# State decays without a biasing product in a recurrent-attention kernel: exponentials on each half of the rows, and a new order of work

## The chip, the core and the metric

The kernel runs on one core of one Trainium2 chip. A core has TensorE (PE), VectorE (DVE), ScalarE (ACT), GpSimd (POOL), and SyncE (SP), which here issues the DMAs. Time is device time in microseconds (us) of one launch; lower is better. Three runs of the kernel before gave 182.21, 182.34 and 183.43 us, a median of 182.34.

## What is computed

A linear attention with data-dependent decay (4 batches, 8 heads, 768 positions, 48 numbers per head), then a mixing layer with two Fourier transforms, a normalization and a two-layer MLP:

```
for t in range(S):
    cur = einsum('bhd,bhe->bhde', u * k[t], v[t])
    y[t] = einsum('bhd,bhde->bhe', r[t], state + cur)
    state = w[t][..., None] * state + einsum('bhd,bhe->bhde', k[t], v[t])

X = fft(fft(x, axis=1), axis=2)            # x: y with the heads side by side, 384 wide
u = x + real(X)
un = (u - mean(u)) / sqrt(var(u) + 1e-6)
out = u + relu(un @ w_ch1) @ w_ch2         # 384 -> 1536 -> 384
```

## The kernel before

**Tiles.** A batch is cut into six chunks of 128 positions, written (batch, chunk) below. For each chunk the tensors w, k, r and v are loaded as 128 x 384 tiles (four loads, 192 KB each, seven buffers per tensor). The logarithm of w (`L`, ACT) is summed along the positions by matmuls with a triangular mask (L799, and L822 for a second kind of sum), and exponentials of these sums scale r and k (L853 on DVE for r, L884 for k). Both are transposed, by PE and an evicting copy (L899, L911), or by a transposing DMA on SP's queue (L889). Then come the scores (L922), a mask (L932), the product with v and with the carried state (L984, L987), and the sum with a diagonal part (L998 on DVE, or L1007 as an fp32 product on PE in batch 0).

**State decay.** Between chunks the state is multiplied by the product of w over the whole chunk, one number per head and feature. The state tile holds two heads stacked: rows 0 to 63 belong to the even head of each of four pairs, rows 64 to 127 to the odd one. `total` makes the exponents in a 128 x 8 strip beside the sums: four small matmuls of `L` with a column of ones (L813) give each pair's sums in two columns, and ahead of them one product of the identity with `PB` (L810, the biasing product) puts -200 into the half that belongs to the other head. The exponential of the strip is then the decay where it belongs, and 0 elsewhere, and can be used as a per-row factor (L967, or L972 and L975 where the state stays in PSUM). In the way `sum_two` the strip lies next to the sums, and one exponential (L826) covers both; in `sum_add` and `sum_key` it has an exponential of its own (`decays`, L831). The last chunk of a batch has no decay.

**Mixing and MLP.** The Fourier transforms are matmuls with tables (L1063 to L1068, then L1107 or L1116). The normalized rows go, transposed, through the MLP in two halves of a batch: L1235 with W1, evicted by ACT or DVE with a ReLU (L1243, L1241), and L1254 with W2, then a last DVE instruction (L1263) and the store (L1274).

**Order.** Every operation is registered with a number; where a step can be done in several ways (`choose`), all of them are registered. `ORDER` lists for each engine which numbers run, in which sequence, and so which way and which engine each step has. An engine works strictly in that sequence. A planner with a cost for each operation laid the lists out; at build time its costs decide only which PSUM bank a tile gets and which waits are written first. 32 warming products (L1321), whose results nobody reads, stand in PE's list as filler. The MLP of one batch is interleaved with the attention of the next ones.

Of the kernel before, what the change touches and what calls it, by code (L numbers as in the profile page):

```python
# [8 lines left out]
ACTF = mybir.ActivationFunctionType  # L9
# [30 lines left out]
        "7 2638 2639 2640 2641 72 98 100 153 101 154 68 151 66 64 123 125 2642 180 181 130 206 183 137 204 "  # L40
        "207 147 200 257 233 259 260 148 190 234 201 243 286 2643 236 287 322 2644 323 320 289 248 296 2645 "
        "2646 437 382 306 2647 384 349 350 2648 402 359 404 352 2649 307 2650 409 438 2651 363 2652 451 452 "
        "2653 2654 2655 2656 695 697 642 698 416 2657 465 453 439 724 750 466 644 645 467 440 2658 468 471 "
        "443 474 446 477 725 2659 478 479 480 483 486 491 454 457 460 503 751 497 498 504 492 505 530 499 "
        "2660 671 2661 493 531 672 2662 518 532 524 513 519 525 526 511 509 2663 728 675 520 553 549 555 547 "
        "551 557 536 748 540 565 559 563 567 777 778 561 538 545 781 685 604 682 594 596 608 602 592 598 735 "
        "801 610 806 606 738 590 600 612 830 583 584 831 576 585 834 577 861 859 862 578 788 569 570 571 791 "
        "888 918 889 614 841 844 916 628 621 892 899 940 941 629 630 1310 901 944 1311 622 1363 1308 969 1361 "
        "623 951 1364 615 1333 1335 1416 1417 616 1386 1341 970 1348 961 962 963 977 964 978 979 980 965 966 "
        "981 982 2664 971 1414 983 984 985 986 987 988 972 973 974 1469 1025 1470 1059 1060 1026 1027 1061 "  # L50
        "991 2665 1388 1102 1527 992 993 1439 1170 1103 1528 1136 2666 1137 1104 1441 1138 1171 2667 1172 "
        "1401 1095 2668 1097 2669 1494 1093 1394 1447 1225 1217 1215 1467 1227 1525 1213 1231 1235 1219 1554 "
        "1223 1233 1555 1492 1457 1454 1404 1351 1221 1229 1500 1558 1237 1582 1238 1244 1507 1245 1510 1251 "
        "1246 1239 1252 1974 1606 1979 1607 1565 1567 2029 1253 2030 1610 1264 1270 2027 1262 1278 1280 2014 "
        "1260 1272 1274 1276 2135 2136 1617 1258 1268 1266 1296 1627 2060 2007 1628 1297 1643 2133 1644 1645 "
        "1629 1646 1630 1647 1648 1631 1632 1635 1649 1650 1651 2080 2085 2067 1652 1636 1653 1637 1654 1718 "
        "1638 1639 1640 1289 1684 1719 1752 1753 1754 1720 1685 1686 1290 1291 1775 2017 1836 2070 2120 1298 "
        "1776 1837 1838 1777 1282 2166 2113 1283 1802 1284 2191 2196 1803 1804 2173 2248 1893 1891 2176 1885 "
        "1901 1895 1883 1881 1879 1887 1899 1889 2123 1897 1910 1911 1917 1918 2224 2276 1903 2231 1919 2233 "
        "1904 1912 1905 2293 1944 2283 1926 1924 2301 1928 2302 1930 2303 2309 2304 2310 2294 1934 1938 2295 "  # L60
        "2311 2296 2312 2297 2313 2314 2298 2315 2316 2317 2318 2319 2305 2320 1936 2372 2306 1932 2373 2374 "
        "2449 2517 2418 2338 2375 2450 2339 2419 2340 2518 2341 1940 2483 2484 2451 2420 1962 1946 1948 2519 "
        "2520 1949 1942 1963 1955 2452 1964 1956 2485 1957 2486 1950 2545 2551 2549 2565 2561 2553 2547 2563 "
        "2557 2559 2567 2555 2576 2583 2569 2570 2577 2584 2571 2578 2585 2604 2596 2598 2594 2590 2612 2600 "
        "2610 2602 2592 2608 2606 2614 2621 2628 2622 2623 2615 2616 2629 2630 2633 2634 2635"),
    "act": (
        "0 17 18 19 97 150 73 112 102 155 203 165 65 124 126 182 121 174 67 69 218 256 208 271 261 235 202 "
        "381 319 149 288 324 280 334 391 343 385 351 403 405 308 400 641 313 694 58 709 699 747 375 428 646 "
        "449 656 489 464 490 752 507 501 495 514 512 496 680 677 554 534 528 556 548 558 529 764 566 800 665 "
        "560 539 546 783 718 562 786 605 523 508 568 603 502 535 817 607 516 808 809 611 517 601 613 543 832 "  # L70
        "858 771 863 873 915 790 824 919 890 925 843 882 1360 544 853 1307 942 1312 934 1413 1322 1375 1365 "
        "910 1331 1334 1336 1418 1387 1524 960 1466 967 1430 968 975 990 1471 976 1389 1350 1384 1440 1031 "
        "1065 997 1096 1098 1495 1437 1529 1449 1218 1226 1228 1539 1481 1232 1214 1581 1403 1216 1220 1234 "
        "1236 1493 1224 1222 1456 1973 1490 1100 1176 1230 1108 1587 1142 1211 1591 1997 1509 1548 2026 1101 "
        "1608 1981 1982 1988 2031 1212 1600 1271 2041 2132 1279 1263 1265 1261 1273 1281 1275 1519 1277 2016 "
        "1259 2137 2050 1267 1269 1626 1576 2079 1633 2147 1655 2087 2094 2088 1634 2190 2103 1642 1656 2069 "
# [1278 lines left out]
```

## Time and profile before

| | |
|---|---|
| median of 3 runs | 182.34 us |
| the profiled execution | 182.32 us |
| its span in the trace | 180.2 us |
| ACT busy | 72% of the span |
| POOL busy | 62% of the span |
| granted TensorE clock | 1.0 |

The engines work side by side, so busy shares do not add up to the time. What sets the time is the chain of waits: followed back from the last instruction, at each step to the thing that released it. PE matmuls are pipelined: a matmul of 384 columns is shown with some 0.326 us, but the next one starts 0.16 us after it, so distances from start to start are the ones to count with. A load's issue on SP's queue and its landing are two events; the profile shows a median of 3.8 to 4.0 us between them for the four input tensors.

### The profile page before, as it was taken

How to read it: one execution, taken by the hardware profiler on the slowest of the kernel's cores; microseconds unless marked ns; L12 is line 12 of the kernel's file. 1: busy time of each engine (PE TensorE's matmuls, PEld its weight loads, DVE VectorE, ACT ScalarE, POOL GpSimd, SP SyncE). 2: the span in 40 equal slices, each digit the busy share in tenths (PEclk: the TensorE clock that was granted, in tenths of full speed). 3: DMA queues.
4: the chain of work that ended last, by engine and by line, in shares of the span. 5: the costliest groups of instructions: out<-in, count | busy, mean ns of one | idle time of the engine just before them, and what ended most of it. 6: DMA issues, size and time to landing. Idle time of an engine off the chain costs nothing.

```text
span 180.2 us, 4569 instructions
## 1 busy us (share of the span) xinstructions
PE 172.6 (96%) x1704; PEld 113.9 (63%) x1704; DVE 155.7 (86%) x372; ACT 130.2 (72%) x311; POOL 111.0 (62%) x140
## 2 busy tenths in 40 slices
PE   5988899999999999999999999999999999999994
PEld 2455566766666576866676766665666776656663
DVE  7699999779998899999999999799999966882543
ACT  3989979589899686899997994986981754290500
POOL 2437779697464588599899865898988070310000
PEclk9999999999999999999999999999999999999999
DMA  5999998998998989999899999999973213304113
GB/s 118 209 209 204 178 200 169 183 208 163 171 206 173 211 166 241 202 204 210 191 216 187 232 161 210 233 160 196 217 162 51 91 44 63 135 4 100 39 58 131
DMA packets 117303, 29.29 MB, mean 163 GB/s; under 512 B 112545, under 2 KB 117282, under 8 KB 117282
## 3 DMA queue, kind: packets, MB, share of 16 engines
q1 hardware_dynamic: 115698, 26.65, 73.5%
q0 software_dynamic: 1584, 2.36, 7.7%
q8 instruction: 13, 0.21, 0.5%
q14 instruction: 8, 0.07, 0.1%
HBM read 23.59 MB, written 4.72 MB: 157 GB/s over the span
## 4 chain that ended last, share of the span: by engine, by line
PE 78%; DVE 7%; DMA 5%; ACT 4%; SPq 2%; issue 2%; POOL 1%; DVEq 0%; POOLq 0%; ACTq 0%
PE bank L1254 23%; PE bank L1235 23%; PE bank L1107 4%; PE bank L922 3%; PE bank L1063 3%; DMA in_v<-in_v_dram 3%; PE bank L911 3%; PE bank L1321 2%; PE bank L987 2%; DMA in_w<-in_w_dram 2%; PE bank L799 2%; PE bank L984 2%; PE bank L959 2%; SPq L889 1%; DVE ah L932 1%
## 5 line engine op out<-in xcount | busy, mean ns | idle before, releaser
L1254 PE MATMUL bank<-w,ht 128*128 128x384 bf16 (+2 forms) x300 | 52.8, 319 | 0.0
L1235 PE MATMUL bank<-unt,w 128*128 128x384 bf16 x288 | 52.0, 326 | 0.0
L1243 ACT ACTIVATE ht<-bank 128x384 bf16<-128x384 f32 x70 | 31.2, 497 | 13.2 <-PE bank L1235 13.0
L1254 PEld LDWEIGHTS bank<-w,ht 128*128 128x128 bf16 x300 | 27.5, 98 | 15.4
L1235 PEld LDWEIGHTS bank<-unt,w 128*128 128x128 bf16 x288 | 27.0, 98 | 15.7 <-DVE ah L932 0.2
L932 DVE TENSOR_TENSOR ah<-bank,msk 128x512 bf16<-128x512 f32 x42 | 27.4, 682 | 0.2 <-PE bank L922 0.2
L578 POOL TENSOR_TENSOR rkh<-in_k,e 128x384 bf16<-128x384 f32 x19 | 19.0, 1002 | 7.2 <-ACT e L840 4.9
L1263 DVE SCALAR_TENSOR_TENSOR osb<-bank,rstd,uf 128x384 f32<-128x384 f32 (+2 forms) x25 | 14.7, 596 | 9.0 <-PE bank L1254 9.0
L578 POOL TENSOR_TENSOR vtd<-in_v,dc 128x384 f32<-128x384 f32 x22 | 18.1, 830 | 5.7 <-DVE rk L578 4.1
L578 POOL TENSOR_TENSOR rk<-in_r,in_k 128x384 f32<-128x384 f32 x18 | 17.9, 1001 | 0.0
L578 POOL TENSOR_TENSOR rk<-rk,ub 128x384 f32<-128x384 f32 x17 | 16.9, 997 | 0.8 <-DVE rk L578 0.5
L1241 DVE TENSOR_SCALAR ht<-bank 128x384 bf16<-128x384 f32 x26 | 13.7, 547 | 2.9 <-PE bank L1235 2.9
L601 ACT ACTIVATE rkt<-bank 128x512 bf16<-128x512 bf16 (+1 forms) x19 | 14.5, 781 | 1.1 <-PE bank L911 1.1
L592 ACT ACTIVATE lb<-in_w 128x384 bf16<-128x384 f32 x24 | 12.3, 521 | 3.0 <-DMA in_w<-in_w_dram 2.9
L592 ACT ACTIVATE vb<-in_v 128x384 bf16<-128x384 f32 x23 | 11.9, 522 | 2.2 <-DMA in_v<-in_v_dram 2.2
L578 POOL TENSOR_TENSOR xf<-sd 128x384 bf16<-128x384 f32 (+1 forms) x9 | 8.9, 999 | 7.4 <-DVE xf L578 5.0
L871 DVE TENSOR_REDUCE dc<-rk 128x8 f32<-128x384 f32 (+1 forms) x24 | 12.5, 526 | 0.1
L853 DVE TENSOR_TENSOR rkh<-bank,in_r 128x384 bf16<-128x384 f32 x21 | 11.5, 547 | 0.4 <-ACT bank L852 0.4
L998 DVE TENSOR_TENSOR x<-bank,vtd 128x384 f32<-128x384 f32 x21 | 11.4, 549 | 0.2 <-POOL vtd L578 0.2
L826 ACT ACTIVATE e<-bank 128x392 f32<-128x392 f32 (+1 forms) x18 | 8.8, 497 | 3.4 <-PE bank L813 2.6
L852 ACT ACTIVATE bank<-bank 128x384 f32<-128x384 f32 x21 | 10.1, 486 | 1.7 <-PE bank L799 1.6
L987 PE MATMUL bank<-vb,ah 128*128 128x48 bf16 x192 | 11.1, 183 | 0.0
(185 smaller groups left out, 373.2 us busy)
## 6 DMA issues: line engine op xcount, KB each, us to landing
in_w<-in_w_dram SPq DMA_DIRECT2D x24, 192.0 KB, 3.8
in_r<-in_r_dram SPq DMA_DIRECT2D x24, 192.0 KB, 3.8
in_k<-in_k_dram SPq DMA_DIRECT2D x24, 192.0 KB, 3.9
in_v<-in_v_dram SPq DMA_DIRECT2D x24, 192.0 KB, 4.0
out_dram<-osb SPq DMA_DIRECT2D x23, 192.0 KB, 2.8
w<-in_moe_w_ch_dram POOLq DMA_DIRECT2D x2, 576.0 KB, 8.6
w<-in_moe_w_ch_dram POOLq DMA_DIRECT2D x1, 1152.0 KB, 11.1
out_dram<-osb SPq DMA_DIRECT2D x1, 128.0 KB, 1.7
```

What stands on the lines that cost most here:

```text
L578: return lambda e: e.tensor_tensor(out=o, in0=a, in1=b, op=f)
L592: return lambda e: e.activation(o, a, f, **kw)
L601: {"act": lambda e: e.activation(o(), i(), ACTF.Copy), "dve": lambda e: e.tensor_copy(out=o(), in_=i())}, **kw)
L853: op("dve", v_1(DM), lambda e: e.tensor_tensor(out=rh[:, :, 0:D], in0=ps(tce)[:, 0:DM].rearrange("t (h d) -> t h d", d=D), in1=rt[:, :, :] ...
L871: op("dve", v_1(H * m), lambda e: e.tensor_reduce(out=dc[:, :], in_=rku[:, :, 0:m], axis=mybir.AxisListType.X, op=ALU.add), r=[("RK", i2)] ...
L932: masked[n].append(op("dve", v_1(512), lambda e: e.tensor_tensor(out=ah[:, x:H:2, :], in0=ps(bk)[:, :].rearrange("p (h t) -> p h t", t=128 ...
L987: ins = e.matmul(ps(ty)[:, D * h:D * h + D], ah[:, h, :], vb[:, h, :], start=first and not ype, stop=True, skip_group_check=True)
L1235: ins = e.matmul(ps(t)[:, 0:384], W1[:, m, 256 * (j // 2) + j % 2:256 * (j // 2) + 256:2], unt[:, :, m, :], start=(m == 0), stop=(m == NM ...
L1241: {"dve": lambda e, j=j, t=t, ht=ht: e.tensor_scalar(out=ht[:, j, :], in0=ps(t)[:, 0:384], scalar1=su, scalar2=0.0, op0=ALU.mult, op1=ALU. ...
L1243: "act": lambda e, j=j, t=t, ht=ht: e.activation(ht[:, j, :], ps(t)[:, 0:384], ACTF.Relu, scale=su)},
L1254: ins = e.matmul(ps(t)[:, 0:hi - lo], ht[:, j, 128 * x:128 * x + 128], W2[:, j, lo:hi], start=(j == 0), stop=(j == NJ - 1))
L1263: op("dve", v_1(hi - lo) + 64, lambda e: e.scalar_tensor_tensor(out=o[:, lo:hi], in0=ps(t)[:, 0:hi - lo], scalar=rstd[:, kb:kb + 1], in1=u ...
```

## The change

The choice `sum` gets a second version of each of its three ways, for all chunks but the last of a batch. In it `total` leaves the biasing product out, and the decays are made by two exponentials, one on rows 0 to 63 of the even columns and one on rows 64 to 127 of the odd columns. The other halves of the strips in the three `E2` buffers are filled with 0 once at the start, by DVE. In `sum_two`, the exponential over the sums then covers 384 columns instead of 392. The planner's figure for a load goes from 998 to 1040 in batch 2 and 1075 in batch 3, and all five lists are new. In the new lists 7 of the 20 chunks use the second version; 13 keep the biasing product.

```diff
-               w=[("in", n, i)], sem="in_%s%d" % (n, i), xfer=998)
+               w=[("in", n, i)], sem="in_%s%d" % (n, i),
+               xfer=998 if b < 2 else 1040 if b < 3 else 1075)
...
+        for i in range(NB):
+            op("dve", 40, fill(E2[i][:, DM:DM + H], 0.0), r=["E20"] if i else [], w=["E20", ("E2", i)])
...
-        def total(t):
+        def total(t, bias=True):
 
             def tot(e):
-                e.matmul(ps(t)[:, DM:DM + H], IDB[:, :], PB[:, :, :].rearrange("p h x -> p (h x)"), start=True,
-                         stop=False, skip_group_check=True)
+                if bias:
+                    e.matmul(ps(t)[:, DM:DM + H], IDB[:, :], PB[:, :, :].rearrange("p h x -> p (h x)"), start=True,
+                             stop=False, skip_group_check=True)
                 for h in range(HP):
                     ins = e.matmul(ps(t)[:, DM + 2 * h:DM + 2 * h + 2],
-                                   L[:, 2 * h:2 * h + 2, :].rearrange("t h d -> t (h d)"), ONE[:, :], start=False,
+                                   L[:, 2 * h:2 * h + 2, :].rearrange("t h d -> t (h d)"), ONE[:, :], start=not bias,
                                    stop=True, skip_group_check=True)
...
+        def sum_two(bias=True):
             tci = g.tile("a")
...
+            total(tci, bias)
+            ne = DM if last or not bias else DM + H
             op("act", a_ps(ne), lambda e: e.activation(E2[i2][:, 0:ne], ps(tci)[:, 0:ne], ACTF.Exp), r=[tci],
                w=[("E2", i2)])
+            if not bias:
+                decays([("E2", i2)], False, tci)
...
+        def decays(w, bias, t):
+            if not last and not bias:
+                for x in range(2):
+                    op("act", a_ps(4) + 20, lambda e, x=x: e.activation(
+                        E2[i2][64 * x:64 * x + 64, DM + x:DM + H:2], ps(t)[64 * x:64 * x + 64, DM + x:DM + H:2], ACTF.Exp),
+                       r=[t, "E20"], w=w)
+            elif not last:
                 op("act", a_ps(H) + 20, lambda e: e.activation(E2[i2][:, DM:DM + H], ps(tce)[:, DM:DM + H], ACTF.Exp),
                    r=[tce], w=w)
...
-        g.choose(("sum", b, c), sum_two, sum_add, sum_key)
+        g.choose(("sum", b, c), sum_two, sum_add, sum_key, *([] if last else [lambda: sum_two(False), lambda: sum_add(False),
+                                                                                     lambda: sum_key(False)]))
```

`sum_add` and `sum_key` hand `bias` on in the same way. Of the five lists, SP's from the 84th place on (counted from 0) is shown: before, 2075 is the w load of chunk (3,2), 2131 the v load of (3,3), and 2006, 2059, 2165, 2112, 2223, 2275 are the transposing DMAs of (3,0), (3,1), (3,3), (3,2), (3,4), (3,5). In the new list these are 2350, 2422, and 2265, none, 2472, 2403, 2546, 2598.

```
before:
1210 2024 2128 627 634 2130 2186 2006 2059 2077 1243 2075 2129 2076 1250 2078 1257 2243
2165 2112 2131 1765 2188 2187 2245 2244 1295 2189 1288 2223 2275 1302 2246 1876
...
after:
1373 2350 2566 2282 2284 2283 2419 2351 2265 1413 2421 1420 2420 2352 1406 2353 2493 2495
2472 2403 2422 2008 2494 2567 2569 2568 1451 2496 1465 2546 2598 2119 1458 2166
...
```

In all lists numbers from 33 on move up by three, and by sixteen more for every chunk registered before that is not the last of its batch, so that the two versions can be compared place by place. The first places of SP's list are 77 70 75 71 74 79 78 before (w of (0,1), w of (0,0), r of (0,0), u, k of (0,0), r and k of (0,1)) and 78 80 81 77 74 82 73 after (r of (0,0), w and k of (0,1), k of (0,0), u, r of (0,1), w of (0,0)). The k load of (0,5) is at place 23 before (93) and 22 after (96).

Counted over the lists, before and after: chunks with the second cumulative product (L822) 18 and 20; chunks of batch 0 with the fp32 product on PE (L1007) 3 and 2; chunks transposed by DMA 6 and 5; evictions of transposes on DVE 5 and 10, of them 1 and 7 of the 128 x 512 kind; warming products 32 and 32, of them after the first MLP matmul 6 and 8.

More of the change, by code (lines that the diff above doesn't have):

```diff
@@ L817, in total @@
             if not last:
-                op("pe", mm(1, 5), tot, r=["ONE", "IDB", "PB0", "PB", ("LB", i2)], w=[t])
-        def sum_two():
+                op("pe", mm(1, 4 + bias), tot, r=["ONE", "IDB", "PB0", "PB", ("LB", i2)], w=[t])
+        def sum_two(bias=True):
             tci = g.tile("a")
```

16 lines of the change are left out of this document (6 added, 10 removed), and 139 rows, old and new, of the table ORDER.

## Prediction

> **What bounds the kernel now.** I read the page first, then the chain of waits in order of time, then the timeline of PE (TensorE) around its gaps, then the busy times by stage.
>
> ```profile
> span 180.2 us, 4569 instructions
> PE 172.6 (96%) x1704; PEld 113.9 (63%) x1704; DVE 155.7 (86%) x372; ACT 130.2 (72%) x311; POOL 111.0 (62%) x140
> PE 78%; DVE 7%; DMA 5%; ACT 4%; SPq 2%; issue 2%; POOL 1%; DVEq 0%; POOLq 0%; ACTq 0%
> ```
>
> The profiled execution took 182.32 us, its span 180.2, so 2.1 us lie outside; the median of three runs is 182.34, so nothing has to be rescaled. PE carries 78% of the chain. The last stretch shows how firmly:
>
> ```profile
> 154.19 5.85 PE bank L1235 x36
> ...
> 171.74 5.89 PE bank L1254 x48
> 177.73 0.35 DVE osb L1263
> ```
>
> 36 matmuls of 384 columns in 5.85 us are 0.1625 us each, start to start, with nothing between. The timeline shows where this spacing is broken after the MLP begins:
>
> ```profile
> 41.40 0.81 PE L1235 MATMUL bank<-unt,w 128*128 128x384 bf16 x4
> ...
> 111.82 0.50 PE L1063 MATMUL bank<-ss,xf 128*128 128x193 bf16 x4
> 113.05 0.32 PE L799 MATMUL bank<-lb,msk 128*128 128x384 bf16 x1 [0.72 <-ACT lb L592]
> ...
> 123.05 0.48 PE L1107 MATMUL bank<-dtm,hcr 128*128 128x384 bf16 x2
> 123.80 0.34 PE L959 MATMUL bank<-vb,rkh 128*128 128x96 bf16 x4 [0.27 <-ACT st L601]
> ```
>
> From the first MLP matmul at 41.40 there are two real gaps. The four products at 111.82 are done issuing at about 112.16 (half of a 384-column spacing each), the next starts at 113.05: 0.89 us lost. The two at 123.05 end at 123.38, the next starts at 123.80: 0.42 us. Both are late loads:
>
> ```profile
> 105.20 2.17 SPq L889
> 107.43 0.58 SPq L624
> 108.06 0.63 SPq L1274
> 108.73 3.62 DMA in_w<-in_w_dram
> 112.38 0.53 ACT lb L592
> 113.05 0.32 PE bank L799
> ...
> 117.65 0.49 SPq L889
> 118.20 4.62 DMA in_v<-in_v_dram
> 122.84 0.53 ACT vb L592
> ```
>
> SP's queue stood 2.17 us at a transposing DMA (L889), whose operands were not ready; the w load of chunk (3,2) (batch 3, chunk 2) waited behind it and landed at 112.3. Then the v load of (3,3), again behind an L889, landed at 122.8. So after 41.4 the time is PE's queued work plus 1.3 us; what else can be won is in the start-up, or by less work. DVE is the second bound, by stage:
>
> ```profile
> 0.00:20.00 20.00, 16.60 (x148) 9.45 (x148) 17.47 (x61) 15.18 (x28) 9.44 (x22) 1.00 0.92 181
> 20.00:40.00 20.00, 19.45 (x236) 13.64 (x235) 18.09 (x41) 15.95 (x36) 17.11 (x24) 1.00 1.03 192
> 30.00:60.00 30.00, 29.99 (x301) 20.23 (x300) 26.45 (x65) 25.78 (x65) 19.73 (x26) 1.00 1.02 183
> 60.00:105.00 45.00, 45.00 (x527) 31.18 (x526) 44.10 (x94) 39.69 (x95) 39.08 (x43) 1.00 1.00 206
> 105.00:127.60 22.60, 21.55 (x224) 14.30 (x223) 20.68 (x47) 17.97 (x46) 17.08 (x19) 1.00 1.12 195
> ```
>
> After the window and its length stand PE, PEld, DVE, ACT and POOL. DVE is idle for 0.9 us of the 45 between 60 and 105.
>
> **What the change does, read from its lists.** The numbers in the lists count operations as they are registered. The change registers three fills ahead of number 33, and sixteen operations in each of the 20 chunks that are not the last of a batch: 323, so the first of the 32 warming products, 2638, becomes 2961. With this shift both lists can be laid side by side. The new way is taken in 7 of the 20 chunks: (1,0), (1,3), (3,0), (3,1), (3,2), (3,3), (3,4). The rest of the edit is the new order. The two longer load figures are inputs of the planner, and issue no work.
>
> **PE's work.** Prices are start-to-start distances:
>
> ```profile
> 24.07 0.81 PE L1007 MATMUL bank<-vtd,ht 128*128 128x384 f32 x2
> 24.71 0.33 PE L1321 MATMUL bank<-idw,msk 128*128 128x384 bf16 x1
> 24.88 0.33 PE L822 MATMUL bank<-lb,nle 128*128 128x384 bf16 x1
> 25.04 0.61 PE L911 MATMUL bank<-idw,rkh 128*128 128x128 bf16 x8
> 25.48 0.33 PE L1321 MATMUL bank<-idw,msk 128*128 128x384 bf16 x1
> ...
> 30.56 0.17 PE L810 MATMUL bank<-pb,idw 128*128 128x8 bf16 x1
> 30.59 0.24 PE L813 MATMUL bank<-one,lb 128*128 128x2 bf16 x4
> ```
>
> - Biasing product (L810): 0.03 us from its start to the next; 7 fewer: -0.2.
> - Adding v by an fp32 product (L1007): one chunk fewer, 24.07 to 24.71: -0.64.
> - The second cumulative product (L822): 18 chunks before, 20 after, at 0.16: +0.33.
> - Transposes: chunk (3,1) goes from a transposing DMA to PE, 8 products from 25.04 to 25.48: +0.44.
>
> Sum -0.1 us. The removal itself is thus worth 0.2 us in 182.
>
> **ACT's work.** The half exponentials (64 rows by 4 columns) do not stand in the trace; the nearest row is the whole one:
>
> ```profile
> L831 ACT ACTIVATE e<-bank 128x8 f32<-128x8 f32 x4 | 0.7, 173 | 0.1
> ```
>
> At 173 ns each, 14 come and 4 go: +1.7 us of ACT. From below, each could be free if it hid wholly in its neighbour; from above, I double the row to 0.35. I take the row, since a fixed cost has no reason to fall with the rows. The Trainium skill ("ScalarE: Activation LUTs", What ACT_TABLE_LOAD costs) gives an ACTIVATE with immediate scale and bias 186 ns plus 0.833 ns per element of a row, so 189 ns here; its number would make 14 for 4 cost 1.9 us, and it speaks against splitting a row of activations at all. Engine time on ACT is covered by its idle share (28%), and the lists take other evictions off ACT; I enter 0. If that cover is gone, both halves stand ahead of a chunk's state decay on DVE and ahead of the Relu evictions behind them on ACT: 7 x 0.35 = 2.4 us at most.
>
> **The start-up.** Ahead of the last mask of chunk (0,5) the DVE list holds 1.06 us less (27.2 to 26.2, each operation at its group's mean less 75 ns of overlap with its neighbour; the three fills are in it). Chunk (0,5)'s k load moves one place up in SP's queue; chunk (0,0)'s w load goes from place 1 to 6, while (0,1) leads instead. PE's list holds 0.8 us less ahead of the first MLP matmul (warming products included), so as much more after it. PE runs gapless from 24 to 41.4 with warming products as filler, so a shorter list reaches the MLP about 0.8 earlier and the two cancel: 0. Bounds: -1.0 if DVE's 1.06 us and the earlier k load also shorten the first 24 us, where PE is idle for 3.4 of 20; +0.8 if (0,0)'s late w load uses up the shorter list.
>
> **The loads of batch 3.** The w load of (3,2) moves from place 95 to 85 in SP's queue, ahead of the transposing DMAs, of which the second (chunk (3,1)) is gone. Ten places at 0.4 to 1.0 us of issue are more than the 0.89 us it was late: -0.9. The v load of (3,3) stays at place 104, right behind the same two transposing DMAs of (3,3) and (3,2), which wait for DVE and POOL: between 0 and -0.42; I take -0.2.
>
> **DVE's work.** Over the whole list DVE gets 2.1 us more: six more evictions of transposes against four fewer bonus products are the largest items.
>
> ```profile
> L602 DVE COPY rkt<-bank 128x512 bf16<-128x512 bf16 x1 | 0.4, 425 | 0.0
> L578 DVE TENSOR_TENSOR rk<-rk,ub 128x384 f32<-128x384 f32 x7 | 3.8, 554 | 1.5 <-ACT ub L601 1.4
> ```
>
> What matters is where it stands: between the last mask of (0,5) and the r product (L853) of (3,5) there are 4.9 us more (90.6 to 95.5). In the three later windows above DVE has 97.6 - 91.2 = 6.4 us of idle time. The next customer has no slack:
>
> ```profile
> 127.64 0.56 DVE L853 TENSOR_TENSOR rkh<-bank,in_r 128x384 bf16<-128x384 f32 x1 [0.42 <-ACT bank L852]
> 127.44 3.15 SPq L889 DMA_TRANSPOSE rkt<-rkh  x2
> rkt<-rkh SPq DMA_TRANSPOSE x6, 4.0
> 133.43 0.62 PE L922 MATMUL bank<-rkt 48*128 48x128 bf16 x16
> ```
>
> The transposing DMAs of (3,4) and (3,5) leave the queue at 130.6; with the median 4.0 us to land from its own issue the second would land at about 133.4, and PE scores both chunks at 133.43. The new list has PE score them 0.8 us of work later. If DVE uses half of its idle time (3.2 us), it is 1.7 late and PE waits 0.9; if three quarters (4.8), nothing. I take +0.5; ends 0 and 4.9 - 0.8 = 4.1.
>
> **Sum.** 182.3 - 0.1 + 0 + 0 - 0.9 - 0.2 + 0.5 = 181.6 us.
>
> **The rivals.**
> *DVE becomes the bound (slower).* If DVE can use only a quarter of its idle time (1.6 us), since most of it is waiting for operands that come no sooner, it is 3.3 us late at (3,5), PE waits 2.5 for the scores, and that one wait swallows the load gains: 182.3 - 0.1 + 2.5 = 184.7 us. It ends over 1% slower when DVE absorbs less than about 2.1 of the 4.9 us. For it: 0.9 us of idle time in the 45 from 60 to 105. Against: PE has MLP products to fill with, and the order was moved 0.8 us in its favour at that place. The Trainium skill ("Perfetto Trace Analysis", Identifying the Most-Contended Engine) calls matmul busy time a bad measure of headroom and takes weight-load busy time instead; by that, PE at 63% is not the bound and DVE at 86% is, which would make this rival the likeliest. The stretch from 154.19, gapless at 0.1625 us a matmul, says otherwise for this kernel.
>
> *All covers hold (faster).* Both load gaps go (-1.3), DVE keeps up, and the start-up gains the 1.0 of its lower bound: 182.3 - 0.1 - 1.3 - 1.0 = 179.9 us. For it: DVE is 87% busy in the first 20 us and gets less to do there. Against: the first lists change places ((0,1) ahead of (0,0)), so that the saving needs a load order that has not been seen.
>
> *The loads do not come sooner (no change).* DMA is busy for 1.0 to 1.12 of the windows up to 127.6, so a load moved up delays another, and the gap returns at another chunk, with the DVE term: 182.3 - 0.1 + 0.5 = 182.7 us.
>
> That the change does not do what it says holds in part: it removes 7 of 20 biasing products, already in the sum.
>
> **Chances.** The forecast 0.48 (180.7 to 182.7), DVE bound 0.17, all covers 0.18, loads no sooner 0.17. A measurement of this kernel can tell about 1% from no change: 180.5 and 184.2. All of the second rival but nothing of the forecast lies below: faster 0.18. Of the first, 0.15 lies above: slower 0.15. The rest is 0.67. The range from 179.8 to 184.5 leaves out the far half of either tail.
>
> **What would show it.** Right: no PE idle before L799 around 112, and the in_w landing there earlier; 13 L810 and 14 half exponentials near 173 ns; DVE idle between 30 and 127 down to about 2 us; the first L1235 near 40.6. Wrong: a PE wait of over 1 us ended by a transposing DMA or by DVE between 60 and 140, a first L1235 after 41.4, or a new wait for a load in batch 2 or 3.

## The result, and the profile after

Ten executions of the changed kernel have a median of 184.5 us (183.54 to 186.75), ten of the kernel before 182.47 us (181.78 to 185.43). The ratio is 1.0108, with a 95% interval from 1.0072 to 1.0143: the change makes the kernel about 2 us slower. The forecast was 181.6 us, with a range from 179.8 to 184.5; the result stands at its upper end, and the sign was forecast wrong. The profiled execution of the changed kernel took 184.19 us, with a span of 182.4 against 180.2, so 2.2 us of span are to be found. The five executions of the changed kernel with a mean granted clock of 1.0, the profiled one among them, have a median of 183.8 us and the five with 0.99 one of 185.79, against 182.2 to 182.7 us for the kernel before at 1.0 in the comparisons below, so that a part of the 2 us goes with the clock. First the page:

```profile
span 182.4 us, 4578 instructions
PE 173.0 (95%) x1705; PEld 113.7 (62%) x1705; DVE 158.7 (87%) x381; ACT 130.5 (72%) x319; POOL 107.3 (59%) x137
L841 ACT ACTIVATE e<-bank 64x4 f32<-64x4 f32 x14 | 2.3, 165 | 0.2
L817 PE MATMUL bank<-pb,idw 128*128 128x8 bf16 x13 | 2.2, 169 | 0.0
PE 65%; ACT 9%; DMA 8%; POOL 7%; DVE 6%; issue 3%; DVEq 0%; POOLq 0%; ACTq 0%
```

The change does what it says: 14 half exponentials, 13 biasing products left. PE is busy for as long as before (173.0 against 172.6), but its share of the chain falls from 78% to 65%. ACT, DMA and POOL have taken the difference. (Line numbers are higher than before: L1235 is now L1250, L1254 is L1269, L799 is L805, L922 is L937, L932 is L947, L998 is L1013, L853 is L868, L889 is L904.)

**Where the 2.2 us are.** The timeline of PE at the first MLP matmul, which was at 41.40 before:

```profile
41.66 0.62 PE L937 MATMUL bank<-rkt 48*128 48x128 bf16 x16
42.75 0.66 PE L1250 MATMUL bank<-unt,w 128*128 128x384 bf16 x3 [0.47 <-DMA w<-in_moe_w_ch_dram]
```

It starts 1.35 us later, and the last matmul ends at 179.86 against 177.62, 2.24 later. So the start-up loses 1.35 and the rest 0.89. The chain of waits ahead of 42.75 (start, length, what) is not PE's any more:

```profile
27.73 1.00 POOL rk L581
28.73 0.79 POOL vtd L581
29.51 0.55 POOL xf L581
30.07 0.96 POOL rk L581
...
31.05 0.55 DVE dc L886
...
31.99 0.77 DVE vtd L581
...
33.05 9.65 DMA w<-in_moe_w_ch_dram
...
42.75 1.31 PE bank L1250 x7
```

POOL works without a gap, two steps of DVE follow, then POOL issues the first half of W1, which takes 9.65 us. In the kernel before, POOL issued it at 31.62. PE itself had its queue done at about 42.2, so W1 alone accounts for only some 0.6 of the 1.35. Even that is not needed for the loss: in the new order without the fills (below) the first MLP matmul is at 42.71, and PE does not wait for W1 there. The busy times of the two start-ups (window, length, then PE, PEld, DVE, ACT, POOL) show how full the engines are, first before and then after (the rows of before from 0 to 20 and from 20 to 40 stand in the prediction):

```profile
24.00:30.00 6.00, 5.97 (x79) 3.95 (x78) 6.00 (x12) 5.52 (x12) 4.96 (x7) 1.00 0.97 191
```

```profile
0.00:20.00 20.00, 15.92 (x140) 8.98 (x140) 16.82 (x61) 14.56 (x28) 9.53 (x24) 1.00 0.93 184
20.00:40.00 20.00, 18.46 (x231) 12.79 (x232) 18.49 (x43) 16.57 (x38) 15.78 (x21) 1.00 0.99 185
24.00:30.00 6.00, 5.25 (x77) 3.25 (x74) 5.97 (x13) 4.35 (x9) 5.74 (x7) 1.00 0.97 190
```

From 24 to 30 DVE is full before and after, and POOL is now nearly full too (5.74 of 6 us). PE, which was busy for 5.97 of 6 us there, is busy for 5.25. The loss does not begin there: in the first 20 us PE is busy for 15.92 us against 16.60 before, in the next 20 for 18.46 against 19.45. The last sum of batch 0 on DVE (L998, now L1013), on which the transform ahead of the MLP waits, moves from 31.78 to 32.85.

**Behind the first MLP matmul.** The two late loads of before are gone from PE's waits, and others have come:

```profile
123.02 0.40 PE L937 MATMUL bank<-rkt 48*128 48x128 bf16 x8
123.88 0.40 PE L937 MATMUL bank<-rkt 48*128 48x128 bf16 x8 [0.46 <-DMA rkt<-rkh]
```

The eight scores at 123.02 take 0.24 us from start to start, so 0.62 us are lost to a transposing DMA of batch 3. The chain shows what made it late: `POOL rk`, `POOL rkh`, then the DMA, 4.85 us on its way.

```profile
116.98 0.80 POOL rk L581
...
117.89 1.01 POOL rkh L581
...
118.94 4.85 DMA rkt<-rkh
```

Counted as distances between matmul starts less the usual spacing, waits over 0.13 us behind the first MLP matmul are 0.22, 0.89 and 0.43 before, and 0.16, 0.35, 0.14, 0.27 and 0.62 after: 1.54 us both times. The 0.89 us of the rest are therefore the spacing of what stands in PE's list there, which is 0.8 us longer. That is not all needed work: 0.33 us of it are two more warming products, and the tests that move the warming products (below) show that these stand in waits.

### The profile page after: what moved, and what is told of

It reads as the page before. It is cut to its first block, busy times and chain, and to the rows that moved or that the text cites. A ratio compares the mean times of both kernels' runs of the same rounds, so it can differ in the third digit from the quotient of the medians.

```text
span 182.4 us, 4578 instructions
## 1 busy us (share of the span) xinstructions
PE 173.0 (95%) x1705; PEld 113.7 (62%) x1705; DVE 158.7 (87%) x381; ACT 130.5 (72%) x319; POOL 107.3 (59%) x137
## 4 chain that ended last, share of the span: by engine, by line
PE 65%; ACT 9%; DMA 8%; POOL 7%; DVE 6%; issue 3%; DVEq 0%; POOLq 0%; ACTq 0%
PE bank L1269 23%; PE bank L1250 23%; DMA w<-in_moe_w_ch_dram 5%; POOL rk L581 4%; DMA rkt<-rkh 3%; PE bank L937 2%; PE bank L1078 2%; ACT rkt L604 2%; PE bank L1122 2%; POOL rkh L581 2%; PE bank L914 2%; PE bank L1002 1%; PE bank L926 1%; PE bank L974 1%; PE bank L805 1%
## 5 line engine op out<-in xcount | busy, mean ns | idle before, releaser
L1250 PE MATMUL bank<-unt,w 128*128 128x384 bf16 x288 | 52.3, 326 | 0.7 <-DMA w<-in_moe_w_ch_dram 0.5
L1269 PE MATMUL bank<-w,ht 128*128 128x384 bf16 (+2 forms) x300 | 52.7, 319 | 0.0
L1250 PEld LDWEIGHTS bank<-unt,w 128*128 128x128 bf16 x288 | 26.6, 98 | 17.2 <-DMA w<-in_moe_w_ch_dram 0.6
L1269 PEld LDWEIGHTS bank<-w,ht 128*128 128x128 bf16 x300 | 27.1, 97 | 15.0 <-issue 0.2
L947 DVE TENSOR_TENSOR ah<-bank,msk 128x512 bf16<-128x512 f32 x43 | 27.9, 681 | 0.9 <-PE bank L937 0.9
L581 POOL TENSOR_TENSOR rk<-rk,ub 128x384 f32<-128x384 f32 x21 | 20.9, 1000 | 7.1 <-DVE pb L586 3.6
L1278 DVE SCALAR_TENSOR_TENSOR osb<-bank,rstd,uf 128x384 f32<-128x384 f32 (+2 forms) x24 | 14.0, 595 | 8.3 <-DMA out_dram<-osb 6.8
L581 POOL TENSOR_TENSOR vtd<-in_v,dc 128x384 f32<-128x384 f32 x21 | 17.3, 830 | 3.6 <-DVE rk L581 2.5
L581 POOL TENSOR_TENSOR rk<-in_r,in_k 128x384 f32<-128x384 f32 x17 | 16.9, 1000 | 3.5 <-DVE vtd L581 1.7
L581 POOL TENSOR_TENSOR rkh<-in_k,e 128x384 bf16<-128x384 f32 x16 | 16.0, 1001 | 3.6 <-DVE rkh L581 1.9
L581 POOL TENSOR_TENSOR xf<-sd 128x382 bf16<-128x382 f32 (+1 forms) x10 | 10.0, 1002 | 8.7 <-DVE sd L581 4.1
L1013 DVE TENSOR_TENSOR x<-bank,vtd 128x384 f32<-128x384 f32 x22 | 12.1, 549 | 0.9 <-POOL vtd L581 0.6
L868 DVE TENSOR_TENSOR rkh<-bank,in_r 128x384 bf16<-128x384 f32 x22 | 12.0, 548 | 1.0 <-DMA in_r<-in_r_dram 0.6
L595 ACT ACTIVATE un<-uf,agg 128x384 bf16<-128x384 f32 x19 | 11.1, 616 | 1.6 <-DVE agg L1159 1.6
L833 ACT ACTIVATE e<-bank 128x392 f32<-128x392 f32 (+1 forms) x20 | 9.8, 491 | 2.6 <-PE bank L820 2.4
L581 POOL TENSOR_TENSOR uf<-uf,xf 128x191 f32<-128x191 f32 x6 | 3.5, 589 | 13.6 <-DVE uf L581 7.4
```

What stands on the lines that cost most here:

```text
L581: return lambda e: e.tensor_tensor(out=o, in0=a, in1=b, op=f)
L595: return lambda e: e.activation(o, a, f, **kw)
L947: masked[n].append(op("dve", v_1(512), lambda e: e.tensor_tensor(out=ah[:, x:H:2, :], in0=ps(bk)[:, :].rearrange("p (h t) -> p h t", t=128 ...
L1013: op("dve", v_1(DM), lambda e: e.tensor_tensor(out=xb[:, c, 0:DM], in0=ps(ty)[:, 0:DM], in1=vflat, op=ALU.add), r=[ty, ("VTD", n % 4)], w= ...
L1250: ins = e.matmul(ps(t)[:, 0:384], W1[:, m, 256 * (j // 2) + j % 2:256 * (j // 2) + 256:2], unt[:, :, m, :], start=(m == 0), stop=(m == NM ...
L1269: ins = e.matmul(ps(t)[:, 0:hi - lo], ht[:, j, 128 * x:128 * x + 128], W2[:, j, lo:hi], start=(j == 0), stop=(j == NJ - 1))
```

## Experiments

Each was timed against the kernel before on the same chip, in five rounds. Ratios have their 95% interval behind them. Numbers in lists are those of the changed kernel.

**Is it the halves or the order?** The changed kernel with all 20 chunks biased again; and the old order with the halves in the same 7 chunks. For chunk (1,0) in PE's list, and in the other direction for the second kernel:

```diff
-... 534 739 446 740 2978 ...
+... 534 727 446 728 2978 ...
```

> The new order with the biasing product back in all 20 chunks and one whole exponential for each strip; lists otherwise as in the changed kernel. If the new order costs the time (theory), it stays where the changed kernel is, about 2.0 us over the kernel before, with 7 x 0.03 = 0.2 us more on PE and 1.7 us less on ACT: ratio 1.009 to 1.013. If the two half exponentials cost it (rival: ACT's extra fixed cost on the path, at most 2.4 us), it falls back to the kernel before: ratio 0.998 to 1.003.

> The order of the kernel before, with the half exponentials and no biasing product in the same 7 chunks, the halves right behind the exponential that they belong to. Theory (the order costs the time): no change, 0.2 us less on PE, ratio 0.997 to 1.002. Rival (the half exponentials cost it): 1 to 2 us slower, ratio 1.005 to 1.012.

The new order with the bias back: 184.19 us, ratio 1.0094 [1.0059, 1.0128]. The changed kernel's loss is there without any half exponential, so the new order loses the time without them. It is not a test of the halves alone: with other exponentials the planner also lays the tiles into other PSUM banks. The old order with the halves: 186.47 us, 1.0219 [1.0180, 1.0259], which nobody expected. It was 4 us slower: its first MLP matmul came at 42.25, 0.85 us late, and the other 3.2 us of its span were lost behind that. So the three fills, which it also held, were tried alone.

**The fills.** The old order with the three fills and no halves; the old order with the halves and no fills (the biased chunks of batch 0 leave the zeros); the new order without fills.

```diff
 "dve":  ... 16 37
+33 34 35
 50 30 ...
```

> The kernel before with nothing of the change but the three fills, which stand in DVE's list right behind the two instructions that make PB, early in the start-up. All 20 chunks keep the biasing product. If the fills caused what the halves in the old order lost (186.47 against 182.3 us, with the whole start-up 0.5 to 0.8 us later), this kernel is slower too: 183 to 184.5 us, and its first MLP matmul is near 42.2 instead of 41.4. If the half exponentials caused it all, it stays at 182.3 to 182.6, and the first MLP matmul at 41.4.

> The old order with the half exponentials in the same 7 chunks, and without the three fills: the chunks of batch 0 keep the biasing product, and their exponentials leave the zeros in all three strips. Theory that the fills' place in the start-up was the loss: 182.3 to 182.8 us, first MLP matmul at 41.4. Rival, that the halves themselves delay ACT (each waits for the end of the one before it) and with it PE around 52 us and 113 us, as in the run with the fills: 184.5 to 186 us, first MLP matmul at 41.4 and 3 us of PE gaps behind it. In between, both have a share.

> The changed kernel without the three fills (the zeros are left by the biased chunks of batch 0); lists, banks and planned waits are the same otherwise. If the fills hold up DVE and POOL in the start-up: first MLP matmul 0.2 to 0.5 us earlier and 184.0 us or less. If DVE has room there, or the order of the start is what costs: 184.3 to 184.5, as the changed kernel.

Fills alone in the old order: 185.0 us, 1.0127 [1.0078, 1.0176]. Halves without fills: 183.53 us, 1.0039 [1.0007, 1.0071]. New order without fills: 184.75 us, 1.0115 [1.0072, 1.0159], so there they cost nothing. 0.33 us of fills that cost 2.3 us need an explanation. The traces show two places. The one in the start-up, where the first MLP matmul moves from 41.40 to 42.27, is in the timeline of POOL, first the kernel before, then the old order with the fills:

```profile
7.79 0.20 POOL L589 MEMSET lb<- 128x128 bf16 x1
```

```profile
10.97 0.20 POOL L592 MEMSET lb<- 128x128 bf16 x1 [3.06 <-DVE rk L581]
11.27 0.52 ACT L595 ACTIVATE lb<-in_w 128x384 bf16<-128x384 f32 x1 [0.83 <-POOL lb L592]
```

A memset of POOL waits 3.06 us for a product of DVE with which it has no data in common, and the logarithm of w on ACT waits for the memset. The wait was put there at build time: the planner lets each POOL instruction wait for the DVE instruction that its timetable has ahead of it (L297 of the changed file; the section on the kernel named only banks and the sequence of waits). With the fills in the timetable, the memset got behind a later DVE instruction, and many PSUM tiles into other banks. The second place is behind the first MLP matmul, where 1.6 us more are lost. PE waits for evictions on DVE where the kernel before has no gap:

```profile
53.15 0.66 PE L1250 MATMUL bank<-unt,w 128*128 128x384 bf16 x3 [0.65 <-DVE ht L1256]
54.07 1.15 PE L1250 MATMUL bank<-unt,w 128*128 128x384 bf16 x6 [0.26 <-DVE ht L1256]
```

From 51.5 to 54.1 these waits come to 1.6 us from start to start. The other banks are a likely cause of them; that was not tried apart. The test keeps the fills in the program and takes them out of the timetable, so that every bank and every other wait is as before. They are no longer chained to each other either, and take 0.10 us together instead of 0.33:

```diff
-            op("dve", 40, fill(E2[i][:, DM:DM + H], 0.0), r=["E20"] if i else [], w=["E20", ("E2", i)])
+            op("dve", 0, fill(E2[i][:, DM:DM + H], 0.0), w=[("E2", i)])
```

> The kernel before with the three fills at the same place in DVE's list as in the run that gave 185.0 us, but free in the planner and not chained to each other, so that every PSUM bank and every wait of a POOL instruction on DVE is as in the kernel before. In the run with the planned fills, one memset of POOL waited 3.06 us for the fortieth DVE instruction (10.97 instead of 7.79 us), and ACT behind it 0.83 us. Theory that the fills cost only through the waits that the planner laid out differently: 182.4 to 182.8 us, the memset at 7.8 to 8.1. Rival, that 0.2 to 0.3 us of DVE in the first 5 us are worth 2 us: 184.5 to 185 us.

182.01 us, 0.9979 [0.9948, 1.0010], and the memset is back:

```profile
7.97 0.20 POOL L592 MEMSET lb<- 128x128 bf16 x1
```

So the fills themselves cost nothing that can be measured; what the planner built around them, waits and banks together, cost 2.3 us. (Of this trace only the memset's place is read: the granted clock is 0.83 between 10 and 20 us.) In the old order with halves, the fills' plan is thereby the larger part of the loss. The smaller, 0.85 us, stays without fills. There the halves stand in the chain, on ACT in batch 3:

```profile
109.73 0.39 ACT e L833
110.14 0.18 ACT e L841
110.34 0.17 ACT e L841
110.54 0.52 ACT vb L595
111.07 0.50 ACT ht L1258
```

```profile
111.71 0.40 PE L937 MATMUL bank<-rkt 48*128 48x128 bf16 x8 [0.69 <-ACT ht L1258]
```

This chain has no free place for the pair: 0.40 us pass from the first half to the next step, where in the kernel before the same columns ride in the exponential of the sums (392 columns instead of 384). At its end PE waits 0.69 us for a ReLU eviction. But the gap of 0.89 us at the w load, at 113.05 before, is not in this kernel, so the wait is not simply added. And a wait that is new stands at 89.51, with no half between 56 and 101 us; the old order with the fills alone, which has no half at all, has it too, at 92.25:

```profile
89.51 0.38 PE L926 MATMUL bank<-idw,rkh 128*128 128x128 bf16 x4 [0.35 <-DVE rkh L868]
```

```profile
92.25 0.38 PE L926 MATMUL bank<-idw,rkh 128*128 128x128 bf16 x4 [0.35 <-DVE rkh L868]
```

From start to start it is worth 0.5 us. So some 0.5 of the 0.85 us are more likely the plan's than the halves'; the two were not tried apart.

**The late loads, and the warming products.** The old order with the w load of (3,2) ten places earlier and the v load of (3,3) ahead of the transposing DMA; the same with the six late warming products moved into the start-up; the new order with its eight moved.

```diff
 "sp": ... 2281 1373
+2350
 2283 2419 ... 1406
-2350
 2420 ... 2566
+2422
 2472 2403
-2422
 2008 ...
```

The new order's eight products went two each ahead of 149 and 218 (scores of (0,0) and (0,1)), 166 (the fp32 product of (0,0)) and 739; the old order's six as their expectation says.

> The kernel before with two places changed in SP's list alone: the w load of (3,2) ten places earlier, and the v load of (3,3) ahead of the transposing DMA of (3,3). The two PE gaps of 0.89 and 0.42 us at 112 and 123 were ended by these loads. If they are worth what I put them at: 181.0 to 181.5 us, faster than before. Rival, that a load moved up delays another load or the transposes behind it, so that the gap turns up elsewhere (as the changed kernel's late gaps did): 182.2 to 182.6 us.

> The kernel before with the two loads moved (which gave 182.1 against 182.68 us), and its six warming products behind the first MLP matmul moved into the start-up, three ahead of the scores of (0,1) and three ahead of those of (0,3), where PE waited 0.6 us each. If the six stand in PE's queue at full price behind the first MLP matmul: 6 x 0.16 = 1 us less than 182.1, so 181.1. Rival, that they stand in waits, as the eight of the changed kernel did: 182.0 to 182.3.

> The changed kernel with the 8 warming products behind the first MLP matmul moved into waits of PE's start-up (two each ahead of the scores of (0,0), the scores of (0,1), the fp32 product of (0,0) and the second cumulative product of (1,0)). Theory (behind the first MLP matmul PE's queued work sets the time): 8 x 0.1625 = 1.3 us faster. Rival (these products stand in waits and cost nothing): no change; the waits show up as idle PE in their places.

The loads: 182.1 us, 0.9957 [0.9930, 0.9984], faster than the kernel before, but by about half of the 1.3 us (0.58 by the medians; from the first MLP matmul to the end of the last one 135.58 us against 136.22). The gap at 123 went; the one at 112 stayed with another name behind it:

```profile
111.29 2.48 DVE L947 TENSOR_TENSOR ah<-bank,msk 128x512 bf16<-128x512 f32 x4
112.03 0.34 PE L805 MATMUL bank<-lb,msk 128*128 128x384 bf16 x1 [0.66 <-DVE ah L947]
```

L805 needs a PSUM bank which the masks on DVE free, and the chain of that kernel is DVE nearly without a break from 104.1 to 112.0. The load had covered this wait. Warming products: 182.07 us, 0.9974 [0.9946, 1.0002], and in the new order 184.41 us, 1.0096 [1.0066, 1.0127]: no gain in either, they stand in waits. The traces of the old order agree: with 0.97 us of warming products gone from behind the first MLP matmul, the stretch from there to the end of the last matmul is 135.62 us, against 135.58 with them.

**What ends the start-up late?** One place after the other was moved in the new order. The first W1 DMA 3.5 us earlier, and then only one place up in POOL's list:

```diff
 "pool": 425
+517 (the first run)
 508 478 379 53
+517 (the second)
 376
-517
 765 518 ...
```

In the first run 518, the second half of W1, also went ahead of 765.

> The changed kernel with the first W1 load issued by POOL about 3.5 us earlier, right after the diagonal part of chunk (0,4), and the second right before where the first was. Theory (the first MLP matmul waits for W1): it starts at about 42.2 instead of 42.75, where PE gets there by itself, and the time falls by 0.4 to 0.6 us. Rival (PE is late for other reasons, or the weights then slow the loads of batch 1): no gain, or up to 1 us slower.

> The changed kernel with the first W1 DMA one place up in POOL's list, ahead of the last xf product of batch 0 (at 31.7 us instead of 33.05, about where the kernel before has it). PE had its scores done at 42.17 us and waited for W1 until 42.75. Theory that W1 costs only these 0.6 us: first MLP matmul near 42.2, 183.9 to 184.0 us. Rival, that W1 ahead of the r and v loads of batch 1 delays them as in the run with W1 3.5 us earlier: the first MLP matmul late or a new gap behind it, over 185 us.

188.0 us, 1.0283 [1.0236, 1.0330], and 186.2 us, 1.0190 [1.0148, 1.0232]. An earlier W1 makes it worse. The chain of the second and its timeline of PE (its granted clock is 0.83 between 10 and 20 us and 1.0 from there on, so that lengths behind 20 us can be compared with other traces, and times of start only roughly):

```profile
32.59 7.34 DMA in_r<-in_r_dram
```

```profile
39.16 0.40 PE L926 MATMUL bank<-idw,rkh 128*128 128x128 bf16 x4 [0.93 <-DVE rkh L581]
```

The r load of (1,0), issued just behind W1, takes 7.34 us where the median of r loads in this part of the changed kernel is 4.1, and PE waits for the chunk. The Trainium skill ("DMA: Bandwidth & Descriptors", Queues, rings and completion order) says that each DMA engine goes round between the queues that have work for it, packet by packet. The measured r load agrees: with a large transfer of POOL's queue in flight it takes nearly twice as long. Nor is that peculiar to this kernel: the loads of v and w that the changed kernel issues right behind W1 take 12.0 and 11.3 us from issue to landing. What the earlier W1 changes is that the r load of (1,0), which PE needs first, now stands behind it.

So the eight loads of batch 1 were put into the sequence of before with W1 up; the set-up (tables ahead of the fills on DVE) and the first seven loads were restored; then set-up and first loads with PE's list changed so that it does not stand for the w load of (1,0); then all of it:

```diff
 "sp", places 0 to 6 and 29 to 36:
-78 80 81 77 74 82 73 ... 859 721 723 790 722 860 792 927
+80 73 78 74 77 82 81 ... 790 721 722 859 723 860 927 792
 "dve", from place 0:
-28 39 46 38 29 24 5 6 42 8 11 48 10 31 12 ...
+23 8 28 6 10 11 9 12 29 32 5 15 13 14 31 ...
 "pe":
-534 739 446 740 2978 794
+534 446 2978 794 739 740
```

> The changed kernel with the set-up (tables, masks, fills; the first 36 places of DVE's list, the first 6 of POOL's) in the sequence of before, so that the sines on ACT are no longer behind nine fills; without the three fills of the strips, which were worth nothing in the new order. In the changed kernel the first sine on ACT starts at 5.33 us against 4.43, and the eviction of u ends at 9.20 against 8.73. Theory that the lost start-up begins there: the first MLP matmul moves from 42.75 to 42.2 or 42.3, and the time from 184.5 to 184.0. Rival, that POOL's list between 24 and 33 us sets the issue of W1 and with it the first MLP matmul whatever the first 9 us do: 184.4 to 184.8.

> The changed kernel with the first seven places of SP's queue in the sequence of before: w of (0,1), w of (0,0), r of (0,0), u, k of (0,0), r and k of (0,1). This is the place from which the prediction's upper bound for the start-up came (w of (0,0) at place 6 uses up the shorter list, +0.8). Theory that the first loads make the start late: PE's first cumulative sum of (0,0) comes earlier, the first MLP matmul moves from 42.75 to 42.2 or less, 183.9 us or less. Rival, that several chains end together at 42.2 to 42.7 (W1 issued behind POOL's list, the r and w loads of batch 1, ACT's evictions), so that no single one moves it: 184.3 to 184.8.

> The changed kernel with the first W1 DMA one place up in POOL's list, as in the run that gave 186.2 us, and with eight loads of batch 1 (places 29 to 36 of SP's queue) in the sequence of before, where r of (1,0) comes third of them instead of fifth. In the run with W1 alone, r of (1,0) was issued at 32.59, behind W1, and took 7.34 us. Theory that W1 and the loads in flight share the same engines, so that W1 can only come early if what PE needs before the MLP is ahead of it: the gaps at 38 and 40 us go, first MLP matmul at 42.0 to 42.6, 183.7 to 184.4 us. Rival, that any earlier W1 starves the loads: the first MLP matmul stays beyond 44 us, 185.5 us or more.

> The changed kernel with three waits of its start-up relieved together: the set-up and the first seven loads in the sequence of before (no fills of the strips), and in PE's list the second cumulative product of (1,0) and its four strip products moved behind the output products of (0,4), a warming product and the cumulative sum of (1,1), so that PE does not stand 0.72 us for the w load of (1,0) at 29.4. W1 stays where it is. Theory that several chains end together: PE is ready for the MLP near 41.5, but W1, issued behind POOL's list at 32 to 33 us and 9.65 us on its way, holds it: first MLP matmul 42.2 to 42.7, 184.2 to 184.7 us. Rival, that PE's own waits were all that counted: 41.5, 183.2.

> The same, with the first W1 DMA one place up in POOL's list and the eight loads of batch 1 in the sequence of before. Theory that the chains have to be relieved together: first MLP matmul 41.6 to 42.3, 183.2 to 183.9 us, below the changed kernel's 184.5. Rival, that POOL is the bound there (W1's issue takes 0.9 us of it ahead of the product that PE waits for at 33): 43 or later, 184.8 us or more.

Set-up: 184.9 us, 1.0103 [1.0046, 1.0161]. First loads: 184.69 us, 1.0121 [1.0092, 1.0151]. W1 with the loads: 185.15 us, 1.0154 [1.0113, 1.0195]; the gaps at 38 and 40 us went, so W1 and the loads are tied, but the first MLP matmul was at 43.67. PE's waits relieved: 184.71 us, 1.0124 [1.0084, 1.0164]. W1 as well: 185.03 us, 1.0138 [1.0109, 1.0167]. None of the five differs measurably from the changed kernel (1.0108 [1.0072, 1.0143]). The chain of the kernel with PE's waits relieved:

```profile
24.47 1.01 POOL rk L581
...
26.50 1.01 POOL rkh L581
...
29.02 0.79 POOL vtd L581
...
30.36 0.95 POOL rk L581
...
31.92 0.56 POOL xf L581
...
32.61 0.32 PE bank L1083
```

Eight microseconds of POOL, with pauses of at most 0.14 us, and then PE's list without a wait up to the first MLP matmul at 42.27; W1 is not in this chain. So the diagonal part of chunk (0,5) was divided between DVE and POOL as in the kernel before, alone and with all other reliefs:

```diff
 "pool": 454 388 421 484 507
-466 425 508 478 379
+478 425 508 482 379
 "dve":  364
+466
 422 436 488 439
+479
 496 443 493
-479
 447
-482
 500
```

> The changed kernel with chunk (0,5)'s diagonal part as before: the product r x k goes back from POOL to DVE, u x r x k moves up two places in POOL's list, the row sum moves up three places on DVE, and the product with v goes from DVE to POOL. In the traces the last x of batch 0 ends the start-up: 31.78 us before, 32.85 in the changed kernel, and the first MLP matmul follows 9.3 to 10.2 us later in every run. In the changed kernel POOL's chain from 24.2 to 31.0 (u x r x k of (0,5) last), then row sum and product with v on DVE, stand ahead of it. Theory that this is where the start-up's time went: last x at 31.6 to 32.1, W1 issued near 32.2, first MLP matmul at 41.7 to 42.2, 183.6 us. Rival, that DVE's and POOL's work as a whole is the bound and the next step is late instead: last x 32.5 or later, 184.3 us or more.

> The same, with the reliefs of the earlier runs together: set-up and first seven loads in the sequence of before (no fills of the strips), the second cumulative product of (1,0) behind the output products of (0,4) on PE, and the eight loads of batch 1 in the sequence of before; W1 keeps its place in POOL's list. Theory: last x at 31.3 to 32.0, first MLP matmul at 41.3 to 42.0, 183.0 to 183.5 us. Rival: as above, first MLP matmul beyond 42.3, 184.3 us or more.

184.95 us, 1.0116 [1.0063, 1.0168], and 184.99 us, 1.0141 [1.0094, 1.0188]. The trace of the first has a granted clock of 0.91 and 0.92 in the two windows from 10 to 30 us, so its times of start cannot be compared with the others. In the second the rival holds: the last sum of batch 0 is at 32.73, the first MLP matmul at 42.63, and the chain has gone from POOL to DVE, and from 30.87 to PE's own list:

```profile
27.31 0.47 DVE rk L581
27.77 0.46 DVE dc L886
28.23 0.60 DVE ah L947
28.83 0.33 DVE rkt L605
29.16 0.60 DVE ah L947
29.76 0.46 DVE dc L886
30.22 0.61 DVE ah L947
...
30.87 0.34 PE bank L805
```

In the changed kernel POOL's issue of W1 stands 0.73 us for DVE's product with v, a wait of the planner's like the memset's, since the load reads nothing of that product. Here the product is on POOL and the wait is gone, and still W1 is issued at 32.75, behind POOL's other work.

## Why the prediction was wrong, step by step

**The step that failed is the start-up.** It was entered at 0: PE's list holds 0.8 us less ahead of the first MLP matmul and as much more behind it, "and the two cancel". The second half came in size (0.89 us more behind it). The first half did not: the matmul came 1.35 us later instead of 0.8 earlier, which is the prediction's own sign of being wrong ("a first L1235 after 41.4"). 1.35 and 0.89 are the whole 2.2 us. Other traces at a granted clock of 1.0 bear the first number out: in the new order with W1 in its place, six more have the first MLP matmul at 42.3 to 43.4, in the old order without planned fills three more have it at 41.6 to 42.1.

The ground for the 0 was that PE runs gapless from 24 to 41.4, so that a shorter list would get to the MLP sooner. It had the path wrong. PE's stretch holds 17 warming products, which are filler, and a product with data waits until its operands are there. In the new order PE is busy for 0.68 us less in the first 20 us already. The last sum of batch 0 on DVE, which the transform needs, is later too: in the profiles of before and after, the first MLP matmul follows 9.6 and 9.9 us behind it. That is no more than an agreement in time, for the chains of waits do not pass through this sum. DVE's 1.06 us less were counted to the last mask of (0,5). In the new list the row sum and the product with v of the same chunk, both on DVE, stand behind that mask and ahead of the last sum (0.55 and 0.77 us in the chain above); before, the row sum stood ahead of the mask and the product was on POOL. The point of measurement hid what had been moved past it. But with both put back the time did not come back, so this is an error of the count and not shown to be the cause. The upper bound of +0.8 rested on one cause, the w load of (0,0); that load turned out to be worth nothing measurable.

What the new order would need in order to start as early as the old stays open. Fills, set-up, first loads, W1, PE's waits and the division of (0,5) were each tried, and most of them together. Eight variants of the new order lie between 184.4 and 185.1 us, and the chain went from W1 to POOL to DVE, and at its end to PE's list. Engines that are full side by side agree with this, but what the new order does with the microsecond was not found in one place. Whether the planner's waits and banks have a part in it, as they had in the old order with 2.3 us, was not tested by itself.

**PE's work, -0.1.** Right in kind: 13 biasing products are left. PE's busy time rose by 0.4 us of 173, which is too coarse for a term of this size.

**ACT's halves, hidden, 0.** The price was right (165 ns against the 173 taken). In the new order nothing measurable hangs on them: 184.19 us with the bias, 184.5 with the halves, each with its own plan. That the idle share of ACT covers them is not a rule, though. In the old order the same seven pairs, with the plan they bring, cost 0.85 us, within the bound of 2.4 named for a lost cover.

**The loads, -0.9 and -0.2.** The load waits went, as said. But the old order with only these two loads moved gained 0.4% (0.2 to 0.7%), where the two terms make 0.6% and the two gaps 0.7%. The interval does not exclude the terms; the trace shows what was left out: 0.66 us of the 0.89 at 112 were a wait for DVE's masks that lay beneath. The forecast priced a gap at its full width without asking what was next late.

**DVE's work, +0.5.** (DVE's evictions of transposes are five more, not six: seven of 128x512 for one, three of 128x1024 for four.) The wait expected at the scores of (3,4) and (3,5) did not come, although the r product of (3,5) stood at 131.36 against 127.64. A wait of 0.62 us for a transposing DMA came one pair of chunks earlier, with POOL ahead of it. That the size came out is chance: the place and the engine are others. DVE's idle time in the three windows from 30 to 127.6 did not fall to 2 us either:

```profile
30.00:60.00 30.00, 29.37 (x299) 20.04 (x300) 25.66 (x64) 25.67 (x67) 18.16 (x24) 1.00 1.04 185
60.00:105.00 45.00, 45.00 (x522) 31.00 (x520) 44.61 (x97) 37.27 (x89) 38.32 (x43) 1.00 0.97 201
105.00:127.60 22.60, 21.84 (x240) 14.63 (x237) 21.75 (x50) 18.85 (x51) 17.64 (x20) 1.00 0.96 181
```

DVE's busy time is the third number with a count: 97.6 less 92.0 leaves 5.6 us idle, against 6.4 before. The rival "DVE becomes the bound" named 184.7 us, close to what was measured, but by a wait of 2.5 us at (3,5) that the trace does not have.

**The best version** found is the old order with the two loads moved: 0.9957 [0.9930, 0.9984] of the kernel before, without halves or fills.

## What to carry to other kernels

When a list is laid out anew, take the instruction that releases the next stage (here the last sum, not the last mask) as the point up to which you count each engine's work, and count what was moved past it on every engine; a gapless stretch with filler in it does not show that its engine is the bound. A gap that ends with a late load is worth its width less the next wait beneath it. Where a planner sets waits and buffers at build time, an added instruction's price includes the plan it changes: give it no time in the planner first, and see whether the loss is its own.

## What the runs showed that was not expected

Three fills of 0.33 us together cost 2.3 us with one plan (1.0127), and nothing with another in which they take 0.10 us (0.9979); the difference is the plan: a POOL memset at 10.97 instead of 7.97 us in the start-up, and other banks, with 1.6 us of waits for DVE's evictions behind 51.5 us. Issuing one 576 KB load of POOL's queue 1.0 us earlier (at 32.04 against 33.05) cost 1.7 us (186.2 against 184.5), with a load issued behind it that took 7.34 us.

A profile's start-up scatters. With the same lists up to there as the kernel before, the first MLP matmul was at 41.84 in the old order with the two loads moved, against 41.40. With the fills out of the timetable, which add 0.10 us to DVE's work there, it was at 42.94, in a trace with a granted clock of 0.83 between 10 and 20 us. Differences of a few tenths between single traces were therefore not counted as results.
